# Weight casts moved from ScalarE to VectorE, and the feed-forward work of all batches put into one first-in first-out list

## The chip, the cores and the metric

The kernel runs on one core of a Trainium2 chip. The metric is the device time of one execution in microseconds (us). There is one launch and one core.

The engines are TensorE (PE, matmuls; its weight loads are listed as PEld), VectorE (DVE), ScalarE (ACT), GpSimd (POOL) and SyncE (SP). Each works through its own instructions in the order in which the program lists them; a wait at the head of one engine's list holds everything behind it on that engine. PE's accumulators (PSUM) and the staging buffers in SBUF are shared out by pools with a fixed number of buffers, so a write can wait for the last reader of a buffer.

## What is computed

Attention with a squared ReLU in place of a softmax, over 8 batches of 12 heads, 448 positions and 64 columns a head, followed by an RMS norm and a SwiGLU feed-forward of 768 to 1536 to 768 over the 3584 rows.

```python
# per batch and head, S = 448, D = 64
scores = q @ k.T / sqrt(D)
attn   = maximum(scores, 0) ** 2 / S
x      = attn @ v                      # 12 heads side by side: [3584, 768]
# all rows
xn  = x / sqrt(mean(x * x) + 1e-6) * rms_g
g   = xn @ w_gate ; val = xn @ w_val   # 768 -> 1536
out = (g * sigmoid(g) * val) @ w_out   # 1536 -> 768
```

## The kernel before

**Weights.** `load_weights` brings w_gate and w_val in six pieces each of 128 x 1536 fp32 (768 KB) through the pool `wstage`, which has two buffers, by DMAs that GpSimd issues (L110, L115). ScalarE turns each piece into bf16 and multiplies it by rms_g on the way (L111, L116). The next DMA into a buffer waits for the cast that reads it. Then come twelve pieces of w_out (L121), cast by GpSimd (L122).

**Attention.** For each batch `load_qkv` brings q, k and v in two halves (SyncE's queue, L84; pool `stage32`, four buffers) and VectorE casts them (L93, L97). `attention_gen` goes over 6 pairs of heads and one closing step. In a step p it transposes q and k of pair p on PE into `tp` (L138), copies them to `qkT` on VectorE (L144), and then four times: a score block `st` on PE (two matmuls, L151; one PSUM buffer), `r_sb` on ScalarE (ReLU, L160; two buffers), `aT` on VectorE (square, L164), and one pair of matmuls into `oA` and `oB` (L176) for the pair before. At a pair's end ScalarE moves `oA`, `oB` into `xT` (L188) and VectorE adds the squares to `ss_acc` (L190 to L194).

**Norm.** `rms_norm` sums `ss_acc` over the partitions on PE (`ss_ps`, L220), takes the square root on ScalarE (L228, with a table load), the reciprocal on VectorE (L235) and makes six `xn` tiles on VectorE (L238).

**Feed-forward.** It has 12 "gv units" a batch (6 matmuls into `g_ps`, L250, and 6 into `v_ps`, L258; then a sigmoid on ScalarE, L266, and two products on VectorE, L268 and L269, which make one of 12 slices of `hT`) and 8 "out units" (12 matmuls into `o_ps`, L279, moved to `o_sb` by ScalarE, L286; after two of them a DMA on SyncE's queue, L288). `g_ps` and `o_ps` share two PSUM buffers, `v_ps` has one.

**What sets the order.** The code hands out the feed-forward work between attention steps: in batch b's step 0 two out units of batch b-2, in each of the steps 1 to 6 two gv units of batch b-1 and one out unit of batch b-2. Batch 0 has none beside its attention, batch 1 only gv units. After batch 7's attention 28 units are left: 12 gv units of batch 7, then 8 out units of batch 6 and 8 of batch 7. A scheduler in the framework then orders the instructions of each engine by the code's order and by when it reckons operands and buffers to be ready, so instructions move a little among their neighbours.

Of the kernel before, what the change touches and what calls it, by code (L numbers as in the profile page):

```python
# [8 lines left out]
ACT = mybir.ActivationFunctionType  # L9
# [6 lines left out]
def kernel(  # L16
# [87 lines left out]
    def load_weights():  # L104
# [3 lines left out]
        for ft in range(NFT):  # L108
            stg = wstage.tile([128, Dff], FP32, name="stg", tag="stg")
            nc.gpsimd.dma_start(stg[:], wg_src[:, ft, :])  # L110
            nc.scalar.activation(  # L111
                out=wg_bf[:, ft, :], in_=stg[:], func=ACT.Copy, scale=rg[:, ft : ft + 1]
# [3 lines left out]
            nc.scalar.activation(  # L116
                out=wv_bf[:, ft, :], in_=stg2[:], func=ACT.Copy, scale=rg[:, ft : ft + 1]
# [125 lines left out]
    def gv_gen(b, xn, result):  # L243
        hT = hp_pool.tile([128, NNT, S], BF16, name="hT")
        result[0] = hT
        for nt in range(NNT):
            g_ps = ps_g.tile([128, 512], FP32, name="g_ps", tag="g")
            v_ps = ps_one.tile([128, 512], FP32, name="v_ps", tag="v")
            for ft in range(NFT):
                nc.tensor.matmul(  # L250
                    g_ps[:, :S],
                    lhsT=wg_bf[:, ft, nt * 128 : (nt + 1) * 128],
                    rhs=xn[:, ft, :],
                    start=(ft == 0),
                    stop=(ft == NFT - 1),
                )
            for ft in range(NFT):
                nc.tensor.matmul(  # L258
                    v_ps[:, :S],
                    lhsT=wv_bf[:, ft, nt * 128 : (nt + 1) * 128],  # L260
                    rhs=xn[:, ft, :],
                    start=(ft == 0),
                    stop=(ft == NFT - 1),
                )
            s_sb = ffnp.tile([128, S], BF16, name="s_sb")
            nc.scalar.activation(out=s_sb[:], in_=g_ps[:, :S], func=ACT.Sigmoid)  # L266
            t_sb = ffnp.tile([128, S], BF16, name="t_sb")
            nc.vector.tensor_tensor(out=t_sb[:], in0=s_sb[:], in1=g_ps[:, :S], op=ALU.mult)  # L268
            nc.vector.tensor_tensor(out=hT[:, nt, :], in0=t_sb[:], in1=v_ps[:, :S], op=ALU.mult)  # L269
            yield  # L270

    def out_gen(b, hT_result):
        for tb in range(R):
            hT = hT_result[0]
            o_sb = outp.tile([IB, Dm], FP32, name="o_sb")
            for half in range(2):
# [13 lines left out]
                o_sb[:, :],  # L290
            )

    def drain(it, n):
        if it is None:
            return None
        for _ in range(n):
# [70 lines left out]
```

## Time and profile before

| | |
|---|---|
| median of 4 runs | 602.4 us (601.37 to 603.29) |
| the profiled execution: its own time | 602.29 us |
| its span in the trace | 600.5 us |
| PE busy | 542.2 us, 90% of the span |
| VectorE busy | 394.6 us, 66% |
| ScalarE busy | 342.6 us, 57% |
| data moved | 58.71 MB |

Matmuls are pipelined, and a busy PE in this table says only that some matmul was under way: a matmul of 448 columns is shown as lasting about 0.35 us where the next one starts 0.19 us later. So the table gives the engine that is in use, and the starts of instructions in the timeline give the speed.

### The profile page before, as it was taken

Reading aid. Unit: us, or ns where it says so; the run is one execution under the profiler, and the core shown is the slowest. Engines: PE = TensorE matmul, PEld = TensorE weight load, DVE = VectorE, ACT = ScalarE, POOL = GpSimd, SP = SyncE. Lnnn points to the kernel's source line nnn. Section 1 sums busy time; section 2 is a strip of 40 time slices with the busy share of each in tenths; the row PEclk is TensorE's granted clock in tenths of the full one; section 3 lists DMA queues with packets and bytes.
Section 4 is the critical chain, followed back from the end, with each engine's and each line's share of the span. In section 5 each row is a group of like instructions: output and inputs, shape, how many; then the busy total and the mean of one; then the engine's idle time right before and its main releaser. Section 6 shows DMA issues by size and latency. Waiting matters only on the chain.

```text
span 600.5 us, 7973 instructions
## 1 busy us (share of the span) xinstructions
PE 542.2 (90%) x3088; PEld 279.5 (47%) x3088; DVE 394.6 (66%) x730; ACT 342.6 (57%) x485; POOL 28.8 (5%) x43
## 2 busy tenths in 40 slices
PE   1644679999999999999999999999999999969996
PEld 0321223444455545455454544554545545424685
DVE  1653489887868687759767786768775866545300
ACT  0476766756765576646755576557664665532221
POOL 1011255000000000000000000000000000000000
PEclk9999999999999999999999999999999999979999
DMA  9999693131325224150415132422200000000023
GB/s 253 316 336 293 200 272 102 46 104 59 93 69 115 71 64 120 48 133 27 121 43 151 57 93 69 116 70 70 69 24 24 24 24 1 23 24 0 10 84 93
DMA packets 39878, 58.71 MB, mean 98 GB/s; under 512 B 1696, under 2 KB 33952, under 8 KB 39840
## 3 DMA queue, kind: packets, MB, share of 16 engines
q1 hardware_dynamic: 37120, 44.05, 27.2%
q0 software_dynamic: 2720, 14.16, 7.2%
q8 instruction: 24, 0.39, 0.3%
q14 instruction: 14, 0.11, 0.1%
HBM read 47.19 MB, written 11.01 MB: 97 GB/s over the span
## 4 chain that ended last, share of the span: by engine, by line
PE 75%; DMA 8%; ACT 6%; DVE 6%; issue 4%; POOL 0%; POOLq 0%; DVEq 0%
PE o_ps L279 21%; PE g_ps L250 18%; PE v_ps L258 16%; PE st L151 8%; DMA stg<-in_moe_w_gate_dram 8%; PE oA L176 6%; ACT r_sb L160 3%; PE tp L138 3%; PE oB L176 2%; DVE aT L164 1%; ACT wg_bf L111 1%; DVE rinv L235 1%; ACT xT L188 1%; PE ss_ps L220 1%; DVE xn L238 1%
## 5 line engine op out<-in xcount | busy, mean ns | idle before, releaser
L160 ACT ACTIVATE r_sb<-st 112x896 bf16<-112x896 f32 x192 | 175.5, 914 | 62.4 <-PE st L151 52.9
L164 DVE TENSOR_TENSOR aT<-r_sb 112x896 bf16<-112x896 bf16 x192 | 120.7, 632 | 45.7 <-ACT r_sb L160 44.8
L250 PE MATMUL g_ps<-xn,wg_bf 128*128 128x448 bf16 x576 | 140.2, 359 | 5.6 <-DVE xn L238 5.4
L279 PE MATMUL o_ps<-wo_bf,hT 128*112 128x384 bf16 x768 | 141.1, 328 | 0.8 <-DVE t_sb L268 0.8
L258 PE MATMUL v_ps<-xn,wv_bf 128*128 128x448 bf16 x576 | 133.2, 357 | 0.9 <-DVE hT L269 0.9
L279 PEld LDWEIGHTS <-hT 128*112 128x112 bf16 x768 | 96.9, 130 | 33.5 <-issue 7.9
L151 PE MATMUL st<-qkT 64*112 64x448 bf16 x384 | 83.1, 423 | 32.0 <-ACT r_sb L160 24.1
L266 ACT ACTIVATE s_sb<-g_ps 128x448 bf16<-128x448 f32 x96 | 52.2, 544 | 60.1 <-PE g_ps L250 59.6
L286 ACT COPY o_sb<-o_ps 112x384 f32<-112x384 f32 x64 | 30.6, 479 | 93.9 <-PE o_ps L279 93.7
L250 PEld LDWEIGHTS <-wg_bf 128*128 128x128 bf16 x576 | 50.2, 98 | 67.2 <-issue 33.1
L258 PEld LDWEIGHTS <-wv_bf 128*128 128x128 bf16 x576 | 51.9, 98 | 57.9 <-issue 19.0
L151 PEld LDWEIGHTS <-qkT 64*112 64x112 bf16 x384 | 29.2, 129 | 93.9 <-issue 76.7
L268 DVE TENSOR_TENSOR t_sb<-s_sb,g_ps 128x448 bf16<-128x448 bf16 x96 | 59.3, 617 | 20.5 <-ACT s_sb L266 19.5
L176 PE MATMUL oA<-aT,vbf 112*64 112x448 bf16 x192 | 60.5, 392 | 4.7 <-DVE aT L164 4.4
L269 DVE TENSOR_TENSOR hT<-t_sb,v_ps 128x448 bf16<-128x448 bf16 x96 | 59.1, 616 | 7.2 <-PE v_ps L258 3.6
L176 PE MATMUL oB<-aT,vbf 112*64 112x448 bf16 x192 | 63.1, 396 | 0.0
L144 DVE COPY qkT<-tp 128x896 bf16<-128x896 bf16 x48 | 29.8, 621 | 35.5 <-PE tp L138 35.4
L176 PEld LDWEIGHTS <-vbf 112*64 112x64 bf16 x384 | 23.7, 111 | 39.2 <-issue 29.4
L188 ACT CAST xT<-oA 64x448 bf16<-64x448 f32 x48 | 25.2, 524 | 21.4 <-PE oA L176 14.2
L235 DVE RECIPROCAL rinv<-rinv 128x448 f32<-128x448 f32 x8 | 23.6, 2952 | 9.8 <-ACT rinv L228 9.8
L93 DVE CAST qbf<-q 112x384 bf16<-112x384 f32 x64 | 20.3, 353 | 14.8 <-PE tp L138 8.5
L97 DVE CAST vbf<-v 112x1536 bf16<-112x1536 f32 x16 | 15.3, 959 | 22.2 <-PE oB L176 16.4
(31 smaller groups left out, 274.5 us busy)
## 6 DMA issues: line engine op xcount, KB each, us to landing
q<-in_q_dram SPq DMA_DIRECT2D x16, 672.0 KB, 5.0
k<-in_k_dram SPq DMA_DIRECT2D x16, 672.0 KB, 6.2
v<-in_v_dram SPq DMA_DIRECT2D x16, 672.0 KB, 6.7
out_dram<-o_sb SPq DMA_DIRECT2D x32, 336.0 KB, 2.7
stg<-in_moe_w_gate_dram POOLq DMA_DIRECT2D x6, 768.0 KB, 8.1
stg<-in_moe_w_val_dram POOLq DMA_DIRECT2D x6, 768.0 KB, 8.5
stg<-in_moe_w_out_dram POOLq DMA_DIRECT2D x12, 384.0 KB, 3.5
rg<-in_moe_rms_g_dram POOLq DMA_DIRECT2D x1, 3.0 KB, 8.7
```

Of the source, the lines that this page charges most:

```text
L151: nc.tensor.matmul(st[:, hs, :S], lhsT=qkT[pp : pp + D, S + jb * IB : S + (jb + 1) * IB], rhs=qkT[pp : pp + D, 0:S], start=True, stop=True ...
L160: nc.scalar.activation(out=r_sb[:, :, :], in_=st[:, :, :S], func=ACT.Relu, scale=relu_scale)
L164: nc.vector.tensor_tensor(out=aT[:].rearrange("p a s -> p (a s)"), in0=r_sb[:].rearrange("p a s -> p (a s)"), in1=r_sb[:].rearrange("p a s ...
L176: nc.tensor.matmul(oTs[hs][pp : pp + D, :S], lhsT=vbf[:, hl, jb * D : (jb + 1) * D], rhs=aTs[jb][:, hs, :], start=(jb == 0), stop=(jb == N ...
L188: nc.scalar.copy(out=xT[pp : pp + D, p, :], in_=oTs[hs][pp : pp + D, :S])
L250: nc.tensor.matmul(g_ps[:, :S], lhsT=wg_bf[:, ft, nt * 128 : (nt + 1) * 128], rhs=xn[:, ft, :], start=(ft == 0), stop=(ft == NFT - 1),)
L258: nc.tensor.matmul(v_ps[:, :S], lhsT=wv_bf[:, ft, nt * 128 : (nt + 1) * 128], rhs=xn[:, ft, :], start=(ft == 0), stop=(ft == NFT - 1),)
L266: nc.scalar.activation(out=s_sb[:], in_=g_ps[:, :S], func=ACT.Sigmoid)
L268: nc.vector.tensor_tensor(out=t_sb[:], in0=s_sb[:], in1=g_ps[:, :S], op=ALU.mult)
L269: nc.vector.tensor_tensor(out=hT[:, nt, :], in0=t_sb[:], in1=v_ps[:, :S], op=ALU.mult)
L279: nc.tensor.matmul(o_ps[:IB, :OH], lhsT=hT[:, nt, tb * IB : (tb + 1) * IB], rhs=wo_bf[:, nt, half * OH : (half + 1) * OH], start=(nt == 0) ...
L286: nc.scalar.copy(out=o_sb[:, half * OH : (half + 1) * OH], in_=o_ps[:IB, :OH])
```

## The change

There are two edits. The first makes the twelve casts of w_gate and w_val a `tensor_scalar` on VectorE, in place of an activation on ScalarE. The second replaces the two sets of generators by one list of units in order of batch: 12 gv units and then 8 out units of batch 0, then those of batch 1, and so on. The attention of a batch takes units from the head of this list: 2 in step 0 (none for the batches 0 and 1), 3 in each other step, whatever they are. So batch 1's attention also takes six out units of batch 0, and from batch 2 on each attention takes two out units of batch b-2, then twelve gv units and six out units of batch b-1. After batch 7's attention 22 units are left: 2 out units of batch 6, 12 gv and 8 out units of batch 7.

```diff
@@ load_weights @@
-            nc.scalar.activation(
-                out=wg_bf[:, ft, :], in_=stg[:], func=ACT.Copy, scale=rg[:, ft : ft + 1]
+            nc.vector.tensor_scalar(
+                out=wg_bf[:, ft, :], in0=stg[:], scalar1=rg[:, ft : ft + 1],
+                scalar2=None, op0=ALU.mult,
             )
...
-            nc.scalar.activation(
-                out=wv_bf[:, ft, :], in_=stg2[:], func=ACT.Copy, scale=rg[:, ft : ft + 1]
+            nc.vector.tensor_scalar(
+                out=wv_bf[:, ft, :], in0=stg2[:], scalar1=rg[:, ft : ft + 1],
+                scalar2=None, op0=ALU.mult,
             )
@@ the feed-forward: gv_gen and out_gen become lists of closures with the same operations @@
-    def gv_gen(b, xn, result):
+    def gv_units(b, xn, hT_holder):
...
-    def out_gen(b, hT_result):
+    def out_units(b, hT_holder):
...
@@ the loop over batches @@
+    fq = deque()
+
+    def pull(n):
+        for _ in range(n):
+            if not fq:
+                return
+            fq.popleft()()
...
         for _step, _ in enumerate(attention_gen(b, halves, res)):
-            if _step == 0:
-                out_it = drain(out_it, 2)
-            else:
-                gv_it = drain(gv_it, 2)
-                out_it = drain(out_it, 1)
-        gv_it = drain(gv_it, 10**6)
-        out_it = drain(out_it, 10**6)
...
+            pull((2 if b > 1 else 0) if _step == 0 else 3)
         xT, ss_acc = res[0]
         xn = rms_norm(xT, ss_acc)
...
-    for key in sorted(gv_pending):
-        drain(gv_pending[key], 10**6)
-    for key in sorted(out_pending):
-        drain(out_pending[key], 10**6)
+        hT_holder = [None]
+        fq.extend(gv_units(b, xn, hT_holder))
+        fq.extend(out_units(b, hT_holder))
+    pull(10**9)
```

How it moves the instructions, at the three places of which the prediction speaks. First ScalarE in the kernel before, in batch 0's attention, around the last two weight casts (`r_sb` is the ReLU of a score block, `xT` the move of a finished pair of heads):

```order
L111 ACTIVATE wg_bf<-stg,rg 128x1536
L160 ACTIVATE r_sb<-st 112x896
L116 ACTIVATE wv_bf<-stg_177,rg 128x1536
L160 ACTIVATE r_sb<-st 112x896
L188 CAST xT<-oA 64x448
L188 CAST xT<-oB 64x448
L160 ACTIVATE r_sb<-st 112x896 x3
```

The casts stand between the ReLUs of the score blocks; 17 of batch 0's 24 ReLUs are ahead of the last cast. In the changed kernel ScalarE has none of them, and VectorE has them, here at the same place (`aT` is the square of a score block, `sqp` and `ss_acc` the sum of squares, `qbf`, `kbf`, `vbf` the casts of the next batch's q, k, v):

```order
L111 TENSOR_SCALAR wg_bf<-stg,rg 128x1536
L166 TENSOR_TENSOR aT<-r_sb 112x896 x2
L93 CAST kbf<-k_556 112x384 x2
L117 TENSOR_SCALAR wv_bf<-stg_177,rg 128x1536
L166 TENSOR_TENSOR aT<-r_sb 112x896 x2
L97 CAST vbf<-v_558 112x1536
L166 TENSOR_TENSOR aT<-r_sb 112x896
L93 CAST qbf<-q_572 112x384 x2
L192 TENSOR_TENSOR sqp<-xT 128x448
```

The casts now stand between the squares, and 19 of batch 0's 24 squares are ahead of the last one. The casts of batch 1's q, k and v, which mostly stood ahead of this place, now stand around and behind it.

The third place is ScalarE at the end of batch 7's attention, where the square root of the norm (`rinv`) starts the chain to the last gv units. Before:

```order
L188 CAST xT<-oB 64x448
L266 ACTIVATE s_sb<-g_ps 128x448 x2
L286 COPY o_sb<-o_ps 112x384
L228 ACT_TABLE_LOAD
L228 ACTIVATE rinv<-ss_ps,eps_t 128x448
L266 ACT_TABLE_LOAD
L266 ACTIVATE s_sb<-g_ps 128x448 x12
L286 COPY o_sb<-o_ps 112x384 x16
```

and after:

```order
L190 CAST xT<-oB 64x448
L305 COPY o_sb<-o_ps 112x384 x3
L230 ACT_TABLE_LOAD
L230 ACTIVATE rinv<-ss_ps,eps_t 128x448
L305 COPY o_sb<-o_ps 112x384 x2
L272 ACT_TABLE_LOAD
L272 ACTIVATE s_sb<-g_ps 128x448 x12
L305 COPY o_sb<-o_ps 112x384 x8
```

Two out units now stand between the norm's sum and the first of the last gv units, on PE as on ScalarE, and 8 in place of 16 out units stand at the end.

## Rows read from the trace of the kernel before

**Rows 1.** The page, the span in 40 slices of 15 us, tenths busy

```profile
PE   1644679999999999999999999999999999969996
```

**Rows 2.** Engines by stretch: length, busy us of each, clock, DMA share, GB/s

```profile
core 0: us, PE busy (x) PEld busy (x) DVE busy (x) ACT busy (x) POOL busy (x), PEclk, DMA share, GB/s
45.00:60.00 15.00, 6.15 (x26) 2.98 (x25) 5.38 (x9) 9.62 (x9) 1.59 (x3) 1.00 0.99 293
```

**Rows 3.** The chain that ended last, start-up: start us, us, what

```profile
20.78 8.24 DMA stg<-in_moe_w_gate_dram
...
56.80 1.58 ACT wg_bf L111
58.66 6.52 DMA stg<-in_moe_w_gate_dram
```

**Rows 4.** Timeline of the start: start us, us, what, [idle before it, releaser]

```profile
67.49 1.56 ACT L116 ACTIVATE wv_bf<-stg,rg 128x1536 bf16<-128x1536 f32 x1
67.64 0.62 PE L151 MATMUL st<-qkT 64*112 64x448 bf16 x2 [1.92 <-ACT r_sb L160]
...
85.73 1.86 PE L220 MATMUL ss_ps<-ss_acc,ones 128*128 128x448 f32 x2 [0.33 <-DVE ss_acc L194]
...
92.72 0.53 PE L250 MATMUL g_ps<-xn,wg_bf 128*128 128x448 bf16 x1
```

**Rows 5.** Groups of instructions: busy us, mean ns of one, idle before

```profile
L164 DVE TENSOR_TENSOR aT<-r_sb 112x896 bf16<-112x896 bf16 x192 | 120.7, 632 | 45.7 <-ACT r_sb L160 44.8
L269 DVE TENSOR_TENSOR hT<-t_sb,v_ps 128x448 bf16<-128x448 bf16 x96 | 59.1, 616 | 7.2 <-PE v_ps L258 3.6
L97 DVE CAST vbf<-v 112x1536 bf16<-112x1536 f32 x16 | 15.3, 959 | 22.2 <-PE oB L176 16.4
```

**Rows 6.** Timeline of VectorE and GpSimd, where they work side by side

```profile
42.42 1.16 DVE L93 CAST kbf<-k 112x384 bf16<-112x384 f32 x4
43.33 0.53 POOL L115 DMA_DIRECT2D stg<-in_moe_w_val_dram  x1 [1.94 <-ACT wv_bf L116]
...
92.05 3.29 DVE L238 TENSOR_TENSOR xn<-xT,rinv 128x448 bf16<-128x448 bf16 x6
92.49 3.54 POOL L122 CAST wo_bf<-stg 128x768 bf16<-128x768 f32 x1
...
102.28 0.83 POOL L122 CAST wo_bf<-stg 128x768 bf16<-128x768 f32 x1 [1.43 <-DMA stg<-in_moe_w_out_dram]
```

**Rows 7.** Timeline, the norm's sums of batch 1 and of batch 7

```profile
137.72 1.02 PE L220 MATMUL ss_ps<-ss_acc,ones 128*128 128x448 f32 x2
...
527.00 0.91 PE L220 MATMUL ss_ps<-ss_acc,ones 128*128 128x448 f32 x2
```

**Rows 8.** Timeline of PE, a step of batch 7's attention

```profile
507.63 2.11 PE L279 MATMUL o_ps<-wo_bf,hT 128*112 128x384 bf16 x12
...
511.27 0.38 PE L176 MATMUL oB<-aT,vbf 112*64 112x448 bf16 x1
...
517.43 2.11 PE L279 MATMUL o_ps<-wo_bf,hT 128*112 128x384 bf16 x12
```

**Rows 9.** Timeline of PE at the end

```profile
533.33 1.07 PE L250 MATMUL g_ps<-xn,wg_bf 128*128 128x448 bf16 x2 [5.41 <-DVE xn L238]
...
541.77 1.30 PE L258 MATMUL v_ps<-xn,wv_bf 128*128 128x448 bf16 x6 [0.18 <-DVE hT L269]
...
564.63 31.36 PE L279 MATMUL o_ps<-wo_bf,hT 128*112 128x384 bf16 x192
```

**Rows 10.** PE alone by stretch: length, busy us, clock, DMA share, GB/s

```profile
533.00:535.00 2.00, 1.67 (x4) 0.50 0.00 0
```

**Rows 11.** Engines by stretch as in rows 2, early and late in one batch

```profile
280.00:285.00 5.00, 4.95 (x30) 2.50 (x27) 4.79 (x11) 3.94 (x6) 0.00 (x0) 1.00 0.00 0
305.00:310.00 5.00, 5.00 (x36) 2.38 (x34) 2.23 (x5) 3.58 (x6) 0.00 (x0) 1.00 0.00 0
```

**Rows 12.** Timeline, gv units one right behind the other at batch 1's end

```profile
135.71 1.30 PE L258 MATMUL v_ps<-xn,wv_bf 128*128 128x448 bf16 x6 [0.50 <-DVE hT L269]
```

## Prediction before the run

> **What bounds the kernel now.** I read the page's slices first, then the windows, the chain of waits at the start, and the timeline at the places where the chain changes engine. The slices [rows 1] show three parts: a start of about 90 us in which PE is busy less than three quarters of the time, a long middle at 9 tenths or more, and an end of the same kind with one dent at 525 to 540 us.
>
> The start is a chain of transfers. A piece of w_gate is on its way for 8.24 or 6.52 us, the cast on ScalarE takes 1.58, and 0.28 us later the next transfer is issued into the same buffer [rows 3]. From 20.78 to 58.66 us that makes four rounds of 9.47 us each. The DMA engines are full meanwhile, 0.99 at 293 GB/s [rows 2], because q, k and v of the batches 1 and 2 travel beside the weights. ScalarE takes casts and ReLUs in one line, so the score blocks wait too: at 67.64 PE had stood 1.92 us for `r_sb` [rows 4]. The last cast begins at 67.49, the norm's sum of batch 0 at 85.73 and the first gv matmul at 92.72 [rows 4].
>
> The middle is PE's own speed. From the sum of batch 1 to that of batch 7 it is 389.28 us [rows 7], 64.88 a batch. A step there takes 9.80 us from one out unit to the next [rows 8].
>
> At the end PE waits 5.41 us for the first `xn` [rows 9], and then it runs at half clock, 0.50, which is 1.2 GHz [rows 10]. The second gv unit's `v_ps` begins at 541.77, 14.77 us after the sum; the 16 out units take the last 31.36 us, 1.96 each [rows 9], or 0.163 us a matmul of 384 columns and so 0.19 for one of 448.
>
> **The change part by part.** I work against the profiled execution, 602.29 us with a span of 600.5; the median of the runs, 602.4, is the same to 0.1.
>
> The casts. No row shows a weight cast on VectorE. The nearest one is its cast of fp32 to bf16 with the same 1536 columns, 0.96 us [rows 5]; the other end is ScalarE's 1.58 [rows 3]. I take 0.96, the same engine and width. What a cast waits for is new: it stands behind one or two squares of 0.63 [rows 5] that wait for ScalarE. I add 0.6 for this. For the transfer I take 6.52, the shorter of the two rows, because in the new order SyncE's second half of batch 1's k waits for a VectorE cast that stands behind the ninth weight cast, so less travels beside the weights. A round is then 0.96 + 0.28 + 6.52 + 0.6 = 8.36, four rounds save 4 x 1.11 = 4.4 us, and the last cast begins at 63.1. Bounds of a round: two pieces of 768 KB at 293 GB/s need 5.4 us, so 6.6 at the least; at the most it is as long as now. That is 0 to 11 us.
>
> What stands behind the last cast. It took 18.24 us from there to the sum [rows 4], with 7 of 24 ReLUs to go and the closing sums, some 2 us a block. In the new order 5 squares are left: 4.0 less, and 0.6 for the shorter cast, so 13.6 and the sum at 76.7, 9.0 earlier. Against this stand VectorE's casts of batch 1, which now come around and behind the last weight cast: 2 of 0.96 [rows 5] and some 10 of 0.29 (four in 1.16 [rows 6]), together 4.8. I take them as hidden under the wait for the score blocks, as VectorE was busy 5.38 of 15 us there [rows 2]; uncovered they cost up to 4.8. The start's term is **-9.0**, with bounds 0 and -15.
>
> ScalarE loses 12 x 1.58 = 19 us of work, worth nothing by itself: its ReLUs wait for PE and for VectorE's squares, which free the two `r_sb` buffers. Queued behind a weight cast on VectorE are now the squares and `qkT`, for which PE waits. So the stall moves from ScalarE to VectorE, and only its length changes.
>
> Batch 1. It takes six out units in addition: 6 x 1.96 = 11.8. By the order 13 transposes and 2 score blocks also fall behind batch 0's sum, 1.0 more. PE has no free time to put them in (9 tenths from slice 8 on [rows 1]); a few waits such as the 0.50 of rows 12 could be filled. **+12.8**, bounds 11 and 14.
>
> The batches 2 to 7, six times. The same work is done in each. By the order PE changes 75 times between kinds of matmul in place of 77, and matmuls of `oA` and `oB`, which start together as a pair, are torn apart three times less: the `oB` at 511.27 stands alone, between a score block and a gv unit [rows 8], and a lone one needs the 0.19 of a pair. 3 x 0.19 is 0.6 a batch; I take 0.5. What speaks the other way is VectorE. Nine gv units instead of six now come in a batch's first three steps with them, in a stretch where VectorE is already busy 4.79 of 5 us, while later it is busy 2.23 of 5 [rows 11]. A unit costs it two products of 0.62 [rows 5]. **-3**, bounds -6 and +9.
>
> The end. Two out units, 3.9 us, stand between the sum and the first gv matmul, under the 5.41 of waiting [rows 9]; ScalarE's two extra copies follow the square root in its line and delay nothing. Six units were paid for in batch 1: -11.8. PE then waits 1.5 us in place of 5.4. No row shows a wait of that length in the middle, so whether the clock falls is bounded from both sides: from 533.33 to 541.77 PE does 25 matmuls of 448 columns, 4.7 us of work in 8.44, and the most it can win is 3.7, the least 0. The six `xn` take 3.29 us [rows 6] and hold the first units at any clock, so I take 3.0. **-18.7**, bounds -15.7 and -19.4.
>
> Sum: -9.0 + 12.8 - 3.0 - 18.7 = -17.9, span 582.6, and with the 1.8 around it **584.4 us**.
>
> **The rivals.** *The start gives nothing.* The casts wait behind squares that wait for ReLUs, the casts of batch 1 are not hidden, and the sum comes when it came: -9.0 becomes 0, 593.4 us. For it: the DMA engines are full until 60 us [rows 2], and a faster cast moves no byte sooner. Against it: two blocks fewer behind the last cast are in the order, and q, k, v wait their turn. Chance 0.15.
>
> *GpSimd issues late.* A GpSimd cast that ran beside VectorE's `xn` products took 3.54 us, another 0.83 [rows 6], so the two engines do hold each other up. If VectorE's weight casts and `qkT` copies hold the issue of the next piece by one cast, 0.96, each of five rounds loses that, 4.8 us: 589.2. Against it: the issue at 43.33 took 0.53 beside a running VectorE cast [rows 6]. Chance 0.08. This is the rule of the Trainium skill that speaks against the change (SBUF — State Buffer, "Who interferes with whom"): a VectorE copy, cast or `tensor_scalar` in its two-port mode takes the port pair that it shares with GpSimd for the whole instruction, and descriptors that GpSimd writes for its DMAs are then starved. By the rule this rival's 589.2 would be the time; the trace agrees for the 3.54 us cast and not for the issue.
>
> *VectorE falls behind in the dense steps.* 1.5 us a batch more, in place of 0.5 less: 6 x 2 = 12, 596.4. For it: rows 11. Chance 0.10.
>
> *Slower: the single `v_ps` buffer.* A unit's `v_ps` matmuls wait until VectorE has read the unit before, and with three units in a row no out unit lies between. Where units follow each other now, PE waited 0.50 [rows 12]. At 0.50 for 12 units in 7 batches it is 42 us, 626; from 0.21 a unit the kernel is slower than before. Against it: six `g_ps` matmuls (1.13 us) and often a score block lie between two `v_ps` groups, and VectorE's product takes 0.62 [rows 5]; at the end, where VectorE has nothing else, the units keep their pace. Chance 0.05.
>
> **How the numbers follow.** The forecast has 0.62, its own range is 578 to 590. With the rivals at 593.4 and 589.2 inside and the one at 596.4 at the edge, the range is 576 to 595; outside are the slower rival, part of the third, and a start near its lower bound. Two tenths of a per cent is about what a measurement of this kernel can tell from no change. Faster by more has 0.94, the same 0.01, slower 0.05.
>
> **What would show it.** In the profile after: a weight cast on VectorE of 0.96 us; the last near 63 and batch 0's sum near 77 us; sums of later batches 64.4 us apart; from batch 0's sum to batch 1's about 65; from batch 7's sum to the end 54.8 in place of 73.5, with a wait of 1.5 us before the first gv matmul and a clock of 1.00 behind it. I am wrong if the sum of batch 0 stays near 85, if `v_ps` groups wait for `hT` in the middle, or if the clock falls again at the end.

## The result and the profile after

| | before | after |
|---|---|---|
| median | 602.43 us (16 runs, 600.96 to 605.9) | 582.64 us (11 runs, 581.39 to 585.98) |
| profiled execution: its own time | 602.29 us | 582.76 us |
| its span | 600.5 us | 581.0 us |
| ratio after to before | | 0.9672, 95% interval 0.9652 to 0.9692 |

The changed kernel takes 3.3% less. The forecast was 584.4 with a range of 576 to 595. The four terms of its sum are set against the trace by the same marks, the norms' sums `ss_ps`:

| stretch | before | after | measured | predicted |
|---|---|---|---|---|
| start to batch 0's sum | 85.73 | 73.39 | -12.34 | -9.0 |
| batch 0's sum to batch 1's | 51.99 | 66.04 | +14.05 | +12.8 |
| batch 1's sum to batch 7's | 389.28 | 386.13 | -3.15 | -3.0 |
| batch 7's sum to the end | 73.5 | 55.44 | -18.06 | -18.7 |
| span | 600.5 | 581.0 | -19.5 | -17.9 |

Here are the marks in PE's timeline of the kernel after (start us, us, what, and in brackets the idle time before it and what ended it). They answer to [rows 4, 7 and 9].

```profile
73.39 1.82 PE L222 MATMUL ss_ps<-ss_acc,ones 128*128 128x448 f32 x2
...
80.16 0.35 PE L256 MATMUL g_ps<-xn,wg_bf 128*128 128x448 bf16 x1
...
139.43 0.92 PE L222 MATMUL ss_ps<-ss_acc,ones 128*128 128x448 f32 x2
...
525.56 0.92 PE L222 MATMUL ss_ps<-ss_acc,ones 128*128 128x448 f32 x2
526.31 4.06 PE L298 MATMUL o_ps<-wo_bf,hT 128*112 128x384 bf16 x24
531.89 0.36 PE L256 MATMUL g_ps<-xn,wg_bf 128*128 128x448 bf16 x1 [1.52 <-DVE xn L240]
...
536.26 1.30 PE L256 MATMUL g_ps<-xn,wg_bf 128*128 128x448 bf16 x6 [0.72 <-DVE t_sb L274]
537.40 1.30 PE L264 MATMUL v_ps<-xn,wv_bf 128*128 128x448 bf16 x6
...
560.70 15.76 PE L298 MATMUL o_ps<-wo_bf,hT 128*112 128x384 bf16 x96
```

The wait of 5.41 us before the last gv units is now 1.52, with 24 `o_ps` matmuls in it. The second unit's `v_ps` comes 11.84 us behind the sum (14.77 before), and eight out units are left at the end where there were sixteen. In the page's 40 slices, of 14.5 us each (the next fence: PE busy, and the granted clock, in tenths), the dent near the end is an 8 where it was a 6, and the start still has six slices below 9, as in [rows 1].

```profile
PE   1478589999999999999999999999999999998996
...
PEclk9999989999999999999999999999999999999999
```

The start, in the chain of waits of the kernel after (start us, us, what):

```profile
31.62 6.26 DMA stg<-in_moe_w_gate_dram
37.91 1.02 DVE wg_bf L111
...
54.98 5.77 DMA stg<-in_moe_w_val_dram
60.78 1.02 DVE wv_bf L117
61.80 2.16 DVE aT L166 x2
63.96 0.87 DVE vbf L97
...
65.36 0.54 DVE qbf L93 x2
66.20 0.90 DVE qbf L93
```

A cast on VectorE takes 1.02 us, a transfer 6.26 or 5.77, against 1.58 and 8.24 or 6.52 [rows 3]. The gate pieces are issued at 20.43 and, four rounds later, at 51.89, which is 7.87 a round (9.47 before). The last cast begins at 60.78 (67.49 before), and the sum comes 12.61 us later (18.24). Behind the last weight cast the chain is VectorE's all the way, and casts of batch 1's v and q stand in it.

### The profile page after: what moved, and what is told of

Same layout as the page of the kernel before. It is cut to its first block, busy times and chain, and to the rows that moved or that the text cites. A ratio compares the mean times of both kernels' runs of the same rounds, so it can differ in the third digit from the quotient of the medians.

```text
span 581.0 us, 7977 instructions
## 1 busy us (share of the span) xinstructions
PE 535.1 (92%) x3088; PEld 279.3 (48%) x3088; DVE 401.8 (69%) x742; ACT 325.8 (56%) x473; POOL 29.7 (5%) x43
## 4 chain that ended last, share of the span: by engine, by line
PE 79%; DVE 7%; DMA 5%; issue 4%; ACT 4%; POOL 0%; POOLq 0%; DVEq 0%
PE o_ps L298 23%; PE v_ps L264 19%; PE g_ps L256 17%; PE st L153 9%; PE oA L178 7%; DMA stg<-in_moe_w_gate_dram 4%; PE tp L140 3%; ACT r_sb L162 2%; DVE aT L166 2%; PE oB L178 1%; DVE rinv L237 1%; DMA stg<-in_moe_w_val_dram 1%; PE ss_ps L222 1%; DVE qkT L146 1%; ACT xT L190 1%
## 5 line engine op out<-in xcount | busy, mean ns | idle before, releaser
L256 PE MATMUL g_ps<-xn,wg_bf 128*128 128x448 bf16 x576 | 145.4, 357 | 3.0 <-DVE xn L240 1.5
L298 PE MATMUL o_ps<-wo_bf,hT 128*112 128x384 bf16 x768 | 138.6, 329 | 0.0
L298 PEld LDWEIGHTS <-hT 128*112 128x112 bf16 x768 | 94.9, 130 | 35.6 <-issue 14.7
L264 PEld LDWEIGHTS <-wv_bf 128*128 128x128 bf16 x576 | 52.5, 98 | 55.0 <-issue 12.6
L153 PEld LDWEIGHTS <-qkT 64*112 64x112 bf16 x384 | 31.2, 129 | 73.4 <-issue 54.9
L178 PE MATMUL oB<-aT,vbf 112*64 112x448 bf16 x192 | 59.5, 392 | 0.0
L97 DVE CAST vbf<-v 112x1536 bf16<-112x1536 f32 x16 | 15.3, 958 | 20.0 <-PE oB L178 14.3
L192 DVE TENSOR_TENSOR sqp<-xT 128x448 bf16<-128x448 bf16 x48 | 18.7, 389 | 15.1 <-ACT xT L190 14.1
```

The source lines that it names most:

```text
L153: nc.tensor.matmul(st[:, hs, :S], lhsT=qkT[pp : pp + D, S + jb * IB : S + (jb + 1) * IB], rhs=qkT[pp : pp + D, 0:S], start=True, stop=True ...
L178: nc.tensor.matmul(oTs[hs][pp : pp + D, :S], lhsT=vbf[:, hl, jb * D : (jb + 1) * D], rhs=aTs[jb][:, hs, :], start=(jb == 0), stop=(jb == N ...
L256: nc.tensor.matmul(g_ps[:, :S], lhsT=wg_bf[:, ft, nt * 128 : (nt + 1) * 128], rhs=xn[:, ft, :], start=(ft == 0), stop=(ft == NFT - 1),)
L264: nc.tensor.matmul(v_ps[:, :S], lhsT=wv_bf[:, ft, nt * 128 : (nt + 1) * 128], rhs=xn[:, ft, :], start=(ft == 0), stop=(ft == NFT - 1),)
L298: nc.tensor.matmul(o_ps[:IB, :OH], lhsT=hT[:, nt, tb * IB : (tb + 1) * IB], rhs=wo_bf[:, nt, half * OH : (half + 1) * OH], start=(nt == 0) ...
```

## Experiments

Each kernel was run beside the kernel before on the same chip, and the ratio is to that. A difference from the changed kernel in us is against its 582.64. The last three columns of this table are starts in each kernel's trace, in us: of the last cast of w_gate and w_val, and of the sums of batch 0 and batch 1. In e7, which writes every weight cast twice, it is the second of the last two; the first begins at 66.75.

| kernel | median us | ratio to before, 95% | last weight cast | sum, batch 0 | sum, batch 1 |
|---|---|---|---|---|---|
| before | 602.43 | | 67.49 | 85.73 | 137.72 |
| after | 582.64 | 0.9672, 0.9652 to 0.9692 | 60.78 | 73.39 | 139.43 |
| e1 casts only | 595.73 | 0.9881, 0.9855 to 0.9908 | 61.06 | 73.96 | 131.43 |
| e2 list only | 592.43 | 0.982, 0.9786 to 0.9854 | 68.70 | 87.39 | 150.59 |
| e3 before, no load of batch 1 | 596.54 | 0.9904, 0.9878 to 0.993 | 61.51 | 80.26 | 132.75 |
| e10 casts split | 592.15 | 0.9843, 0.9794 to 0.9891 | 69.35 | 86.51 | 148.84 |
| e7 weight casts twice | 587.94 | 0.9763, 0.9738 to 0.9789 | 68.22 | 75.43 | 144.02 |
| e4 four weight buffers | 581.21 | 0.9655, 0.963 to 0.968 | 53.18 | 73.16 | 137.16 |
| e9 after, no load of batch 1 | 578.15 | 0.9601, 0.9578 to 0.9624 | 59.74 | 71.95 | 134.87 |
| e14 w_out casts twice | 586.1 | 0.9724, 0.9687 to 0.976 | 60.84 | 76.09 | 145.50 |
| e13 w_out on ScalarE | 595.76 | 0.988, 0.984 to 0.9921 | 60.84 | 83.69 | 152.22 |
| e5 empty wait | 589.79 | 0.9787, 0.9757 to 0.9818 | 63.62 | 75.65 | 142.07 |
| e6 four under the wait | 580.35 | 0.9638, 0.9608 to 0.9669 | 60.20 | 72.66 | 139.63 |
| e11 = e4 and e6 | 578.44 | 0.96, 0.9564 to 0.9636 | 53.14 | 74.32 | 137.91 |

In e5, e6 and the changed kernel the program is the same up to batch 7, and yet the first sum lies between 72.66 and 75.65, and the last weight cast between 60.20 and 63.62. So a shift of the start by less than about 3 us in one trace proves nothing by itself.

### The two edits apart (e1, e2)

```diff
# e1: kernel before, load_weights only
-            nc.scalar.activation(out=wg_bf[:, ft, :], in_=stg[:], func=ACT.Copy, scale=rg[:, ft : ft + 1])
+            nc.vector.tensor_scalar(out=wg_bf[:, ft, :], in0=stg[:], scalar1=rg[:, ft : ft + 1], scalar2=None, op0=ALU.mult)
# and the same for wv_bf; e2: the changed kernel with these lines turned back
```

> The kernel before with the first edit alone: the twelve casts of w_gate and w_val on VectorE, the old hand-out of the feed-forward units. If the two edits add up, the start is that of the changed kernel: last weight cast near 60.8 us, batch 0's sum near 73.4 (85.73 before). The 21 transposes and 4 score blocks that the order then puts behind this sum are paid in batch 1: from the sum of batch 0 to that of batch 1 about 54.3 (51.99 before, 66.04 in the changed kernel, of which six out units are 11.8). The middle stays at 64.88 a batch and the end at 73.5, with the wait of 5.41 and the clock of 0.50. Total 602.4 - 12.3 + 2.3 = 592.4. Rival: batch 1's 14.05 is wholly the list's, and the moved transposes fall into gaps: 590.1. Rival: the gain of the start needs the list (out units that fill batch 1): near 600.

Measured: 595.73, 3.3 more than the theory and between its two rivals. The sum of batch 0 came at 73.96, as expected, so the start's gain belongs to the casts. From there to the sum of batch 1 it took 57.47 us and not 54.3, and the next stretch 63.47 in place of 65.02; the miss is in the first of these. The middle stayed at 64.93 a batch and the end at 73.54, with a wait of 5.41.

> The changed kernel with the weight casts back on ScalarE: the second edit alone. If the edits add up: batch 0's sum near 85.7 as before, batch 1 longer by six out units, 11.8, so 63.8 between its sums, the batches 2 to 7 at 64.36 each (-3.15 in all), the end 55.4 (-18.06). Total 602.4 + 11.8 - 3.15 - 18.06 = 593.0. Rival: batch 1's whole 14.05 is the list's: 595.2. Rival: the middle's gain of 3.15 belongs to the casts and not to the list: 596.1, with 64.88 a batch.

Measured: 592.43. The stretches are 63.20 (expected 63.8), six of 64.30 (64.36), and 55.2 at the end (55.4). So the middle's gain and the end's belong to the list alone, and of batch 1's +14.05 the list makes +11.21, six out units. The rest of the 14.05, 2.84, comes with the casts: e1 has 5.48 more in batch 1 than the kernel before, and 1.55 less in the next stretch, without a single extra unit. Added up, the two edits alone give a ratio of 0.9701 (0.9881 + 0.982 - 1) against 0.9672 together. Their intervals, 0.0027 and 0.0034 to a side, hold that difference, so no interplay is shown.

### Why the weights come sooner (e3, e10)

The prediction rested the shorter round on two things, a cheaper cast and fewer transfers beside the weights. The second shows in SyncE's queue. Before, the issues between 25 and 52 us:

```profile
28.01 0.36 SPq L84 DMA_DIRECT2D k<-in_k_dram  x1
32.86 0.31 SPq L84 DMA_DIRECT2D v<-in_v_dram  x1
42.32 0.31 SPq L84 DMA_DIRECT2D q<-in_q_dram  x1
43.61 0.31 SPq L84 DMA_DIRECT2D k<-in_k_dram  x1
```

and after, in the same view, the last issue ahead of this stretch and the next one:

```profile
24.10 0.31 SPq L84 DMA_DIRECT2D q<-in_q_dram  x1
52.71 0.31 SPq L84 DMA_DIRECT2D k<-in_k_dram  x1
```

Each of these transfers waits for a staging buffer that a VectorE cast has to empty, and in the changed kernel that cast stands behind the weight casts. To take the transfers away without moving a weight cast (VectorE's casts of batch 1's q, k and v go with them):

```diff
# e3: kernel before
-        halves = halves0 if b == 0 else load_qkv(b)
+        halves = halves0 if b <= 1 else load_qkv(b)
```

> The kernel before, in which batch 1's attention uses the q, k and v of batch 0 over again, so that the loads and casts of batch 1's q, k and v are left out. In the kernel before, four transfers of q, k and v were issued between 28 and 44 us, beside the weights, 672 KB each: 2.75 MB, or 9.4 us at 293 GB/s; in the changed kernel none between 24.1 and 52.7. Theory: that is most of the difference in the rounds of the weight transfers. Then the rounds fall here from 9.47 to 8.4 with the casts still on ScalarE (1.57 + 0.28 + 6.0 + 0.6), the last weight cast begins near 63.2 in place of 67.49, and batch 0's sum 4 to 5 us earlier than 85.73. Total about 598. Rival: the casts in ScalarE's line set the round, not the traffic: the last cast stays at 67 to 68 and the sum at 85 to 87; total 601 to 603.

Measured: 596.54. With the casts still on ScalarE (1.57 us), GpSimd's queue shows rounds of 8.18 us, (53.11 - 20.41) / 4:

```profile
20.41 0.53 POOL L110 DMA_DIRECT2D stg<-in_moe_w_gate_dram  x1 [16.71 <-ACT wg_bf L111]
...
53.11 0.53 POOL L110 DMA_DIRECT2D stg<-in_moe_w_gate_dram  x1 [4.46 <-ACT wg_bf L111]
```

The last cast begins at 61.51, 5.98 earlier than before; in the changed kernel it is 6.71 earlier. So without these loads and their casts the weights come about as early as in the changed kernel. But the sum of batch 0, on which the time depends, comes at 80.26, only 5.47 earlier, where the changed kernel's is 12.34 earlier: the traffic is less than half of the start's gain. Where the rest comes from is seen at e9. (e7, below, shows that a cast's length counts too: 1.01 us more made a round 1.19 longer. The two together come to more than the 6.71, so they don't simply add.) The next test is to put half of the casts back on ScalarE, which lets VectorE reach batch 1's casts sooner:

```diff
# e10: the changed kernel, w_val only
-            nc.vector.tensor_scalar(out=wv_bf[:, ft, :], in0=stg2[:], scalar1=rg[:, ft : ft + 1], scalar2=None, op0=ALU.mult)
+            nc.scalar.activation(out=wv_bf[:, ft, :], in_=stg2[:], func=ACT.Copy, scale=rg[:, ft : ft + 1])
```

> The changed kernel with the six casts of w_gate on VectorE and the six of w_val back on ScalarE. Theory: in the changed kernel VectorE's own work bounds batch 0 (busy 38.7 of 45 us between 30 and 75; without batch 1's casts the kernel was 4.5 faster, with twelve casts more 5.3 slower), so six casts fewer on it, 6.1 us, bring the sum of batch 1 about 2.5 us earlier: 580. Rival: what made the start short is that VectorE's queue kept batch 1's loads away from the weights. In this order 32 casts of q and k, where it was 24, stand ahead of the last weight casts, so these loads go out beside the weights again: rounds of 8.5 to 9 us, last weight cast at 64 to 67 in place of 60.8, and a total of 585 to 588.

Measured: 592.15, the rival, and more of it than I gave. SyncE's queue has its four issues beside the weights again, the first and the last of them:

```profile
33.75 0.31 SPq L84 DMA_DIRECT2D k<-in_k_dram  x1
...
44.40 0.31 SPq L84 DMA_DIRECT2D k<-in_k_dram  x1
```

The rounds take 9.43 us ((57.98 - 20.26) / 4), the last weight cast begins at 69.35, and the sum comes at 86.51: the start of the kernel before, with half of the casts on VectorE and less work on it (38.1 us busy in the first 75, 49.3 in the changed kernel). So splitting the casts evenly is worth nothing here (592.15, against 592.43 with all of them on ScalarE). It does not show that the order of the transfers is the only reason, because ScalarE's queue has casts that wait again, too: up to the sum PE waited 15.0 us for `r_sb` and 12.6 for `aT`, against 22.6 and 4.1 in the kernel before and 4.2 and 11.1 in the changed one.

### What bounds the start now (e7, e4, e9, e14, e13)

```diff
# e7: the changed kernel, every weight cast written twice
+            nc.vector.tensor_scalar(out=wg_bf[:, ft, :], in0=stg[:], scalar1=rg[:, ft : ft + 1], scalar2=None, op0=ALU.mult)
```

> The changed kernel, in which VectorE does each of the twelve weight casts twice, so that a cast costs 2.03 in place of 1.01 us. Theory: a round of transfer, cast and next transfer into the same buffer bounds the start, so each of some five rounds takes 1.0 longer: last weight cast near 65 to 66 in place of 60.8, batch 0's sum near 79, total 588. Rival: the DMA engines bound the start (their share is 0.79 to 1.10 there) and the cast is hidden: last cast within 1 us of 60.8, sum and total within 1.5 of 73.4 and 582.6.

Measured: 587.94, the total as expected, but not by the expected path. A round grew by 1.19 us to 9.06 ((59.35 - 23.13) / 4) and the last cast came at 68.22, 7.4 later (its first copy 6.0 later), while the sum of batch 0 came only 2.0 later, with one score block and three transposes fewer ahead of it. Another 2.5 us fell into batch 1. So a later last weight cast does not move the sum one for one.

```diff
# e4: the changed kernel
-    wstage = ctx.enter_context(tc.tile_pool(name="wstage", bufs=2))
+    wstage = ctx.enter_context(tc.tile_pool(name="wstage", bufs=4))
-    hp_pool = ctx.enter_context(tc.tile_pool(name="hpool", bufs=3))
+    hp_pool = ctx.enter_context(tc.tile_pool(name="hpool", bufs=2))
```

> The changed kernel with four staging buffers for the weights in place of two, paid for with two hT buffers in place of three. Theory: two buffers hold the weight transfers back, as a buffer stands idle for the cast and the issue; with four the DMA engines stay full. By the last weight some 16.3 MB have to travel, 55 us at 295 GB/s, so the last transfer lands near 57 and the last cast begins near 57 in place of 60.8; batch 0's sum near 70, total 579 to 580. Rival: four pieces issued at once take the DMA engines from batch 0's q, k and v (1.5 MB more ahead of them, 5.2 us), its attention starts late, and batch 0's sum comes at 76 to 79: 585 to 588. Rival: the DMA engines are the bound with two buffers already: 582 to 583.

Measured: 581.21. The last cast begins at 53.18, 7.6 us earlier, twice what I expected, and the sum of batch 0 at 73.16, where it was. An earlier last weight cast does not move the sum either. VectorE's waits up to 74 us (total, times, longest) show one reason; in the changed kernel this wait is 5.7:

```profile
DVE vbf L97 <- DMA v<-in_v_dram: 10.1, 2, 9.6
```

Four weight pieces travel ahead of batch 0's v, so its attention starts late, which was the rival: the first score block comes at 21.11 where it was at 17.20. That the two effects cancel is argued and not shown by a run. The order of work also puts 13 transposes and one score block more ahead of the sum, and batch 1 is 2.04 us shorter. The gain of 1.4 us lies inside the two intervals.

What is left as a candidate for the bound is VectorE itself, busy 38.7 of the 45 us between 30 and 75 us in the changed kernel. The prediction had taken its casts of batch 1 as hidden.

```diff
# e9: the changed kernel
-        halves = halves0 if b == 0 else load_qkv(b)
+        halves = halves0 if b <= 1 else load_qkv(b)
```

> The changed kernel, in which batch 1's attention uses the q, k and v of batch 0 over again: the loads and casts of batch 1's q, k and v are left out. The prediction took VectorE's casts of batch 1 behind the last weight cast as hidden. The chain of the changed kernel runs through a v cast of 0.87 and two stretches of q casts, 0.54 and 0.90, between 61.8 and 67.1 us. Theory: these 2.3 us are paid, so from the last weight cast to batch 0's sum it takes about 10.3 us in place of 12.6, and the sum of batch 1 comes some 2.3 earlier than 139.43, near 137; total about 580. Rival: hidden; the sum of batch 1 stays at 139 to 140, total 582.6. The last weight cast stays near 60 in both, since only one transfer less travels beside the weights.

Measured: 578.15, 4.5 us less, about all of the 4.8 us that these casts were counted at, and batch 1's sum 4.56 earlier. The last weight cast moved only to 59.74. The casts are not hidden, though the loads that fall away with them may have a part in the 4.5. (The order of work differs too: without the casts, 21 transposes and two score blocks more stand ahead of batch 0's sum. That is why only 1.4 of the 4.56 us show in that sum and the rest in batch 1, and the comparison is at batch 1's sum.)

Set against e3, this run also shows what else the start gained. Neither kernel has loads or casts of batch 1, PE has the same matmuls ahead of batch 0's sum in both, and the last weight cast begins at nearly the same time (61.51 and 59.74). Yet the sum comes at 71.95 in place of 80.26, 8.31 earlier. The medians agree: 596.54 - 578.15 is 18.4 us, of which the list alone gives 10.3 (e2 against the kernel before on its chip, 602.75), so that 8.1 are left for the moved casts. PE's waits up to batch 0's sum (total, times, longest) show where they come from, first e3, then e9:

```profile
PE st L151 <- ACT r_sb L160: 17.7, 13, 2.7
...
PE oA L176 <- DVE aT L164: 3.5, 6, 1.1
```
```profile
PE oA L178 <- DVE aT L166: 8.8, 6, 5.5
...
PE st L153 <- ACT r_sb L162: 4.8, 11, 1.0
```

With the weight casts in its queue, ScalarE delivers the ReLUs late, and the score blocks behind them wait 17.7 us. With the casts on VectorE it is 4.8, while the waits for the squares grow from 3.5 to 8.8. Together that is 21.2 against 13.6, 7.6 of the 8.31. How much of it is the shorter cast and how much that ScalarE no longer waits for pieces (5.2 and 1.0 us in e3) no run separates.

Then the casts of w_out. Two rows of VectorE and GpSimd in the changed kernel, side by side:

```profile
65.92 0.98 POOL L124 CAST wo_bf<-stg 128x768 bf16<-128x768 f32 x1 [0.96 <-DMA stg<-in_moe_w_out_dram]
```
```profile
66.13 0.98 DVE L93 CAST qbf<-q 112x384 bf16<-112x384 f32 x1
...
68.09 0.34 DVE L93 CAST qbf<-q 112x384 bf16<-112x384 f32 x1
```

The q cast at 66.13 ends 0.2 us behind GpSimd's cast and takes 0.98; the one at 68.09, with GpSimd idle, takes 0.34.

```diff
# e14: the changed kernel, every w_out cast written twice
             nc.gpsimd.tensor_copy(out=wo_bf[:, nt, :], in_=stg3[:, :Dm])
+            nc.gpsimd.tensor_copy(out=wo_bf[:, nt, :], in_=stg3[:, :Dm])
```

> The changed kernel, in which GpSimd does each of the twelve w_out casts twice. The w_out casts are needed only where the first out units come, 40 us later, so GpSimd's own time is hidden; the order on the other engines is the same. Between 60 and 100 us of the changed kernel VectorE's squares took 0.764 us on the mean in place of 0.632 (16 of them), its q and k casts 0.506 and 0.426 in place of 0.29 (8 of each): 2.1 + 1.7 + 1.1 = 4.9 us more than elsewhere, 0.4 for each w_out cast. Theory: GpSimd's casts hold VectorE up and VectorE bounds this stretch, so twelve more cost it up to 4.9 us: batch 1's sum 2 to 5 us later than 139.43, total 585 to 588. Rival: VectorE's slow instructions there have another cause, or its time is hidden: 582 to 583.5.

Measured: 586.1, 3.5 more; the sum of batch 1 came at 145.50, 6.07 later, a little over what I gave, and the last weight cast at 60.84, where it was. (The trace is of the slowest of the four runs, 588.47, so its 6.07 is more than the median shows; the interval of e14 and that of the change, which ends at 0.9692, just overlap.) The squares between 60 and 110 us, by their group in the changed kernel, in e14 and in e13 below (busy us, mean ns of one, idle before):

```profile
L166 DVE TENSOR_TENSOR aT<-r_sb 112x896 bf16<-112x896 bf16 x21 | 15.2, 730 | 1.8 <-ACT r_sb L162 1.7
```
```profile
L167 DVE TENSOR_TENSOR aT<-r_sb 112x896 bf16<-112x896 bf16 x18 | 17.2, 962 | 1.6 <-ACT r_sb L163 1.6
```
```profile
L166 DVE TENSOR_TENSOR aT<-r_sb 112x896 bf16<-112x896 bf16 x14 | 8.5, 617 | 7.4 <-ACT r_sb L162 7.4
```

With one GpSimd cast a piece a square takes 0.730 us on the mean, with two 0.962, with none 0.617. So GpSimd's casts hold VectorE up, and the later sum says that VectorE bounds this stretch. The Trainium skill has this as a rule (SBUF — State Buffer, "Who interferes with whom"): VectorE and GpSimd share a port pair, and whichever issues first keeps it for its whole instruction, a product of two SBUF operands being caught as well as a cast. These rows agree with it. Does the gain come by taking these casts off GpSimd?

```diff
# e13: the changed kernel
-            nc.gpsimd.tensor_copy(out=wo_bf[:, nt, :], in_=stg3[:, :Dm])
+            nc.scalar.copy(out=wo_bf[:, nt, :], in_=stg3[:, :Dm])
```

> The changed kernel with the twelve casts of w_out on ScalarE in place of GpSimd. In the changed kernel a q cast on VectorE that ran beside a w_out cast on GpSimd took 0.98 us, where such casts take 0.3 otherwise, and a square 1.25 in place of 0.63. Theory: each w_out cast on GpSimd costs VectorE about 0.6 us, four of them ahead of batch 0's sum and eight behind it, where VectorE also makes the xn tiles; VectorE is the bound up to there, so the sum of batch 1 comes 2 to 4 us earlier than 139.43 and the total is 579 to 581. Rival: ScalarE's casts of some 0.8 us stand ahead of ReLUs and take the gain back: 582 to 584.

Measured: 595.76, 13 us slower, far outside both cases. VectorE's squares are short again, 0.617, and idle in front of them for ScalarE's ReLU. ScalarE's group of these casts from 60 to 110 us:

```profile
L124 ACT CAST wo_bf<-stg 128x768 bf16<-128x768 f32 x12 | 9.9, 831 | 17.0 <-DMA stg<-in_moe_w_out_dram 16.8
```

I had counted the 0.83 us of a cast and left out what a cast waits for. In front of these casts ScalarE stood 16.8 us for transfers, and every ReLU behind them stood too. On GpSimd the casts waited for transfers as well, 13.9 us in the same stretch of the changed kernel, with only further pieces of w_out queued behind them. It is also what the kernel before paid: up to the sum of batch 0 its ScalarE waited 8.6 and 3.3 us for weight pieces, in the view of its waits (`wg_bf` and `wv_bf`, both ended by the transfers).

### The last wait and the clock (e5, e6)

```diff
# the loop over batches; e5 takes 5 units in batch 7's last step, e6 takes 1
-            pull((2 if b > 1 else 0) if _step == 0 else 3)
+            pull((2 if b > 1 else 0) if _step == 0 else (5 if b == B - 1 and _step == HP else 3))
```

> The changed kernel, in which batch 7's last step takes five units in place of three, so that no out unit is left to stand between the last norm's sum and the first gv matmul. The work is the same, only the wait is empty again. Theory: PE waits 5.4 us in place of 1.5, and behind a wait of that length the granted clock is 0.50 for a while, as in the kernel before. The second unit's v_ps then begins 8.4 us behind the first g_ps in place of 5.5: +3.9 + 2.9, total 582.6 + 6.8 = 589.4. Rival: the clock has nothing to do with the length of this wait, only the wait itself comes back, +3.9: 586.5, with a clock of 1.00 behind it. Rival: the norm's chain finishes as much earlier as the square root's table load is ahead of ScalarE's two copies: +2 to +3.

Measured: 589.79 (expected 589.4). The wait is 5.42 again and the clock falls again. PE's timeline of e5, and its windows (length, busy us, granted clock, DMA share, GB/s):

```profile
532.09 0.92 PE L222 MATMUL ss_ps<-ss_acc,ones 128*128 128x448 f32 x2
538.42 1.60 PE L256 MATMUL g_ps<-xn,wg_bf 128*128 128x448 bf16 x3 [5.42 <-DVE xn L240]
...
546.98 1.30 PE L264 MATMUL v_ps<-xn,wv_bf 128*128 128x448 bf16 x6 [0.18 <-DVE hT L277]
```
```profile
538.00:540.00 2.00, 1.58 (x4) 0.50 0.00 0
...
542.00:545.00 3.00, 3.00 (x10) 0.57 0.00 0
545.00:548.00 3.00, 2.67 (x14) 1.00 0.00 0
```

Against that the same windows' view of the changed kernel, behind its wait of 1.52:

```profile
533.00:536.00 3.00, 2.54 (x14) 1.00 0.01 3
536.00:540.00 4.00, 3.73 (x20) 1.00 0.00 0
```

From the first `g_ps` to the second unit's `v_ps` it takes 8.56 us at the half clock of 0.50 (1.2 GHz) and 5.51 at 1.00. So two units worth 3.9 us of work, moved by a few microseconds, are worth 7.

> The changed kernel, in which batch 7's last step takes one unit in place of three, so that four out units stand between the last norm's sum and the first gv matmul. Theory: the 1.52 us of waiting goes, and as the six xn tiles are all made by then, the first gv units no longer go at the pace of the xn products: 18 matmuls at 0.19 are 3.4 us where 5.51 passed. Total 582.6 - 1.5 - 2.1 = 579.0, with no wait over 0.3 us on PE there and a clock of 1.00. Rival: only the wait goes, 581.1. Rival: ScalarE's two further copies of out units get ahead of the square root and delay it by 0.5 us each; then the wait stays and the time is 582 to 584.

Measured: 580.35, 2.3 us less than the changed kernel, between the theory and its weaker rival. PE does not wait for `xn` any more:

```profile
522.16 1.02 PE L222 MATMUL ss_ps<-ss_acc,ones 128*128 128x448 f32 x2 [0.16 <-DVE ss_acc L196]
523.02 7.96 PE L298 MATMUL o_ps<-wo_bf,hT 128*112 128x384 bf16 x48
530.82 1.30 PE L256 MATMUL g_ps<-xn,wg_bf 128*128 128x448 bf16 x6
```

From the sum to the end it takes 56.44 us, less the two units more that lie in it (3.92) 52.5, where the changed kernel needs 55.44: 2.9 less, of 3.6 expected. The medians alone would not settle it: e6's interval, 0.9608 to 0.9669, overlaps that of the change.

### A version faster than both (e11)

e11 is the changed kernel with the edits of e4 and e6.

> The changed kernel with the four weight buffers (and two hT buffers) and with four out units under the last wait, two edits that gave 581.2 and 580.35 alone. They lie 380 us apart and touch no common work, so they should add up: 582.6 - 1.4 - 2.3 = 578.9. Rival: the four buffers' gain was the spread of the start between runs, and this is 580.4.

Measured: 578.44, a ratio of 0.9600 (0.9564 to 0.9636), which does not touch the interval of the change alone (0.9652 to 0.9692). It is 4.2 us faster than the changed kernel and 24 faster than the kernel before. By the medians e6 carries the larger part, and the 2.9 at the end of its trace stand for it; neither edit alone has an interval that is clear of the change's.

## Why the prediction held, step by step

The sum came out 1.8 us off in part by luck: the start gained 3.3 us more than forecast and batch 1 lost 1.25 more, and some of both is the same work moved from one side of batch 0's sum to the other. At batch 1's sum the two terms together are +1.71, where the forecast had +3.8.

**The start, -9.0 predicted, -12.34 measured.** The weight cast was right (0.96 taken, 1.02 measured). The round was put at 8.36 and was 7.87. The step that was too small is the transfer: I took 6.52, the shorter of two rows of the kernel before, and the median from issue to landing is 5.5 (w_gate) and 5.7 (w_val) in the changed kernel, 8.1 and 8.5 in the one before. The reason given for it, that SyncE's transfers wait behind VectorE's weight casts, shows in SyncE's queue, and e3 has 5.98 of the last weight cast's 6.71 us without moving a weight cast. It was there in the forecast, but worth only the difference between two rows of before. The forecast was also wrong to put the relief of ScalarE's queue, 19 us of casts, at nothing by itself. It had rightly said that the stall moves to VectorE and changes its length, but that length is the larger part of the start: PE's waits for `r_sb` and `aT` up to the sum fall from 26.7 us to 15.3, and with the loads out of the way (e3 against e9) the moved casts still bring the sum 8.31 earlier. The rival "the start gives nothing" had a sound argument, that a faster cast moves no byte sooner. It failed because other bytes were moved later, and because the score blocks no longer wait for ReLUs behind a waiting cast.

**Behind the last cast, 13.6 predicted, 12.61 measured**, right for reasons that were partly wrong. That 5 squares are left is in the order. But the forecast set them against 7 ReLUs; like against like it is 8 squares before and 5 after, so one block more is saved than the two that it counted. And the casts of batch 1, taken as hidden because VectorE was busy 5.38 of 15 us [rows 2], are on the chain, and e9 puts their price at 4.5 us. I judged VectorE's room by a stretch of the kernel before, in which it had not yet got the twelve casts. The two errors have opposite signs. e4 and e7 show that by now the last weight cast is not all that the sum waits for.

**Batch 1, +12.8 predicted, +14.05 measured**, just over the bound of 14. The six units cost 11.21 by e2 (11.8 predicted). The rest, 1.0 in the forecast, came out near 2.8, and e1 shows that it comes with the casts, though there it is 5.48. Part of it is the 13 transposes and 2 score blocks behind the sum. That the other part is VectorE's work beside GpSimd's casts there is argued from e9 and e14, which both move this stretch, and not separated from the spread of the start.

**The batches 2 to 7, -3.0 predicted, -3.15 measured.** The forecast counted three pairs of `oA` and `oB` a batch that are no longer torn apart, 0.19 each. In the trace of before, in the batch from 267.67 to 332.60 us, four pairs are torn, such as the one at 296.66 (the next fence, PE's timeline); in the changed kernel's batch from 268.05 to 332.36 it is one. Three times 0.19 is 0.57, and a batch takes 64.93 before and 64.31 after. e2 has the same 64.3 with the list alone, and one torn pair. The match of count and time is the evidence; no run changes the pairs alone.

```profile
296.66 0.35 PE L176 MATMUL oA<-aT,vbf 112*64 112x448 bf16 x1
296.94 0.40 PE L151 MATMUL st<-qkT 64*112 64x448 bf16 x2
297.27 0.38 PE L176 MATMUL oB<-aT,vbf 112*64 112x448 bf16 x1
```

**The rivals of the middle did not come.** In the whole trace after, PE waits 0.24 us before `v_ps`, so neither the single buffer nor VectorE in the dense steps holds it up. The six `g_ps` matmuls between two `v_ps` groups cover the product, as the prediction said against the slower rival.

**The end, -18.7 predicted, -18.06 measured.** The wait of 1.5, the clock of 1.00 behind it and the 3.0 us that this gives back were right: from the sum to the second unit's `v_ps` it takes 11.84 us, and the forecast gives 14.77 - 3.0 = 11.77. e5 confirms that filling the wait is the cause: the whole 6.8 come back in its trace (58.31 us from sum to end, and 3.92 of units fewer in it) when the two units are taken out. The 0.6 that is missing comes behind that: from there to the first of the last out units it takes 23.30 us (537.40 to 560.70) where it took 22.86 (541.77 to 564.63), with one matmul more, 0.19, to do, and the eight out units less were worth 15.6 and not 15.7.

**GpSimd issues late.** It does, in one round. Beside VectorE's casts of k and w_val the issue at 20.43 took 2.36 us, and beside one of v that at 22.96 took 1.23; the eight from 31.62 to 54.98 us took 0.53 to 0.63.

```profile
20.43 2.36 POOL L110 DMA_DIRECT2D stg<-in_moe_w_gate_dram  x1 [16.72 <-DVE wg_bf L111]
22.96 1.23 POOL L116 DMA_DIRECT2D stg<-in_moe_w_val_dram  x1 [0.17 <-issue]
...
51.89 0.63 POOL L110 DMA_DIRECT2D stg<-in_moe_w_gate_dram  x1 [3.59 <-DVE wg_bf L111]
```

In e5 the first of these issues took 0.69, and its round 10.14 us in place of 11.19. So the rival's price, about one cast a round, was right in size, but it was paid in one round and not in five. The rule of the Trainium skill that the prediction set beside it (SBUF — State Buffer, "Who interferes with whom") shows here in these two issues, and much more in GpSimd's casts; the time of 589.2 that the prediction drew from it did not come. The row that the prediction held to agree, the 3.54 us cast of [rows 6], ran beside `xn` products and not beside a VectorE cast; it is a case of what e14 tests and not of a late issue.

## What to carry to other kernels

Before moving a cast to the other engine, ask two things: which transfers wait behind it on either queue, and whose operands stand behind it while it waits for its own. Here leaving out the loads beside the weights, with their casts, brought the first sum 5.47 us forward, and taking the casts out of ScalarE's queue at nearly the same arrival of the weights 8.31; splitting the casts evenly gave it all back. A step that waits for a transfer belongs on an engine whose queue holds nothing that others need, since its wait is paid by all that stands behind it. At a wait on a chain of small operations, put independent matmuls into it; if that keeps PE's clock from falling, it is worth more than its own time, here 6.8 us for 3.9.

## What was not expected of the hardware

- Behind a wait of 5.41 or 5.42 us PE's granted clock was 0.50 for some 6 us, and behind one of 1.52 it stayed at 1.00. But the length of one wait does not tell it all: in the changed kernel the clock was also 0.50 from 82 to 84 us (the next fence: length, busy us, clock, DMA share, GB/s), and the last waits ahead of that are 1.00 us at 78.46 and 0.77 at 79.63.

```profile
82.00:84.00 2.00, 2.00 (x7) 0.50 0.29 81
```

- VectorE's squares took 0.617, 0.730 and 0.962 us on the mean beside none, one and two GpSimd casts a piece. The price is VectorE's, though the casts look like free work on an idle engine.
- The same program's start, up to the first norm's sum, varied by 3 us between executions (72.66, 73.39 and 75.65), while the batches 2 to 6 took 64.3 to 64.6 us each in all three.
- Left open: four weight buffers brought the last weight cast 7.6 us forward and nothing of it reached batch 0's sum. Whether it would with batch 0's v sent ahead of the extra pieces was not tried.
